# Merged streams in steps of two: maxima, value products and convolution transforms of an attention and long-convolution kernel

## The chip, the cores and the metric

The kernel runs as one program on one core of a Trainium2 chip. The metric is the device time of one launch in microseconds (us). Of the kernel before there are three timed runs: 1141.32 (the median), 1143.27 and 1141.15 us. A profile is one further execution, with the hardware's instruction records.

The core has five engines with a queue each, all in program order: PE (matrix products, with PEld for its weight loads), DVE (vector), ACT (activation), POOL (a second, slower vector engine, which also issues some DMAs) and SP (which here issues most DMAs). Products land in PSUM, eight banks of 128 partitions by 512 numbers; the other engines take them out of there.

## What is computed

Two independent halves, written side by side into one output of 2048 by 1152 numbers.

```python
# half A: attention, 32 heads of 18, a window of 256 keys, causal
qkv = x @ wqkv
scores = q @ k.T * 18 ** -0.5, masked to 0 <= i - j < 256
a = concat_heads(softmax(scores) @ v) @ wo
# half B: a convolution over the sequence, one filter of 2048 taps per channel (576 channels)
K = Re sum_n C[d,n] * dB[d,n] * exp(dt A[d,n] * l)
b = irfft(rfft(u, 4096) * rfft(K, 4096))[:2048] + u * Dskip
```

## The kernel before, in words

**Three parts in time.** First the projections `x @ wqkv` (`proj`), the taps of the filters (`tables`) and the first step of a two-step Fourier transform of `u` and of the taps (`s1_u`, `s1_k`) run, the results going to DRAM (`qd`, `vd`, `gx`, `gk`). Then, under a hand-written order, comes `attention` (line 758), which merges the attention with the rest of the convolution. Last, the part of the output product that had to wait for the last heads (`wo_rest`). The change touches only the second part.

**Attention.** There are 16 units (8 groups of 4 heads, 2 halves of the sequence), each cut into 6 items: two chunks `c` of 512 queries by three banks of the `BL` table (line 657). So there are 96 items, and 98 rounds of the loop in line 768. For each unit:

- `gmax` (line 627) finds, for blocks of 32 queries, the greatest score of each query, before the softmax. It copies the queries into a block-diagonal tile `qb` (DVE, line 632). Then for each of 32 blocks PE forms the scores of 4 heads by 2 products (line 640, weights of 128 rows by 64 columns) into one `ring` buffer, and DVE takes the maximum over up to 288 keys (line 643). A transpose on PE (line 648) and a scaling on DVE (line 650) turn the 32 columns of maxima into rows, which SP copies into the query tile (line 653).
- `scores` (line 662) forms an item's transposed scores, in two steps (head pairs `jp`), by products with 64 rows by 128 columns of weights (line 676) into `stp`; ACT takes the exponential into `P` (line 678); after both steps POOL masks the blocks on the window's edge (line 687).
- `values` (line 690) runs two items later: for each of an item's one or two blocks, 4 products (one for each head, 8 instructions in the profile, since a product of 32-bit numbers is two) with 128 rows by 32 columns of weights (line 699), a step of the merge for each block. At the last bank ACT takes the sum out (line 707).
- `norm` (line 724) divides by the sums of the softmax: DVE lines 735, 738, 748, 751, PE line 747 (full-size weights), ACT line 749, POOL's DMAs line 755.

**Convolution.** `conv` (line 484) takes 16 pairs of frequencies, each in two halves `hs` of the channels. For one half: two transforms of `u` (`s2`, line 504, part `tx`, weights 128 by 64), each taken out to `X` by ACT (line 527); the transform of the taps, real part `kr` and imaginary part `ki` (line 504, part `tk`), each multiplied straight from PSUM by two DVE products (lines 530, 531 and 534, 535); POOL adds the terms to `Y` (lines 539, 540). The inverse transform of the half before follows: two products with full-size weights (line 511), each taken out by ACT (line 512) into `ho`, which goes to DRAM `h`. After all 16 pairs, a second loop of 16 passes `qd` reads `h` back (`loadh`, line 551: 4 DMAs on SP's queue, 4 of `u` on POOL's), does the last transform (line 577), adds `u * Dskip` (DVE line 579; POOL line 573 forms the product) and writes the output by 4 DMAs from SP, given to `after` for the next round.

**What sets the order.** Each of these is a Python generator; a `yield` ends a step. `merge` (line 82) always calls the stream that has done the smallest share of its steps, the first in the list on a tie. In each round the list is: `scores` with 2 steps, a part of `gmax` with 5 or 6, `values` with 2, a part of `conv` with 2 or 3 (222 over 96 rounds, line 796), and later the output product `wo_first`, `wo_part`. The order in which the steps are called is the order of the instructions in each engine's queue. `share` (line 102) spreads a total over rounds. `after` and `begin` (lines 114, 118) hold a DMA back to the start of a later round.

**The buffers in between.** All products but `scores` and `values` take their PSUM bank from one pool, `ring`, with three buffers, in turn (`stp` has two of two banks each, `ops` one): a product waits until the buffer used three allocations ago has been read out. `fy` and `fs` hold the convolution's SBUF tiles, two of each name.

## Time and profile before

| what | value |
|---|---|
| median of three runs | 1141.32 us (1141.15 to 1143.27) |
| the profiled execution | 1142.89 us, of which the span of the instructions is 1141.2 us |
| first part (to the filters' transform) | to about 522 us |
| merged part: maxima of the first unit | 522 to 545 us |
| rounds 0 to 81 | 545 to 1004 us |
| rounds 82 to 97 (the convolution's last loop among them) | 1004 to 1112 us |
| the last output products | 1112 to 1141.2 us |
| instructions of line 640, 699, 504, 511 (all on PE) | 1024, 1408, 512, 128 |

How the profile is read: a timeline row gives start, duration, engine, line, operation, the tile written and the tiles read, the weights' shape (rows `*` columns) for PE, the shape of the result, and the number of instructions merged into the row; `[0.41 <-DVE t L535]` says that the engine stood idle for 0.41 us before it and which instruction released it. PE's ends are modelled, and rows overlap a little, so PE's rate is read from start to start. A group's row gives a line's total busy time, the mean duration in ns, and the idle time before it with its releasers. A row of waits gives who waited for whom: the total in us, how often, and the longest. The chain that ended last is followed back from the last instruction, at each step to what released it. In the table by stage each row has, for each engine, busy us and the number of instructions, then the granted clock of PE, the busy share of the DMA engines and GB/s.

### The profile page before, as it was taken

What the parts mean: (1) busy time and instruction counts of PE and PEld (TensorE: products, weight loads), DVE (VectorE), ACT (ScalarE), POOL (GpSimd) and SP (SyncE); (2) the same over time, 40 slices, a digit from 0 to 9 for tenths busy, and PEclk for the clock granted to TensorE, in tenths of its full rate; (3) what the DMA queues carried; (4) which work ended last, traced back from release to release, by engine and by line L of the source; (5) the groups of instructions that cost most, each with busy time, mean ns of one, the idle gap of its engine ahead of it and who ended that gap; (6) DMA issues with size and microseconds to landing.
All of it is one profiled execution on the core that took longest, in us unless ns stands there. A gap on an engine that the chain in (4) does not pass through costs nothing.

```text
span 1141.2 us, 27005 instructions
## 1 busy us (share of the span) xinstructions
PE 921.1 (81%) x10412; PEld 450.9 (40%) x10412; DVE 717.9 (63%) x1805; ACT 624.2 (55%) x955; POOL 519.8 (46%) x618
## 2 busy tenths in 40 slices
PE   1535879887979789885888889889888999987876
PEld 0313436555545555532333333333333444433325
DVE  2879656866785562266667677787776566563344
ACT  1785778777878842231355555655555455544430
POOL 0014324442644330102355556666756555487860
PEclk9957989898989889998599998999999999999888
DMA  9564423433343325885153464544445334287753
GB/s 272 152 192 138 97 50 90 110 87 84 87 106 65 76 56 124 216 252 159 43 163 117 129 184 115 156 132 125 132 127 153 88 125 142 81 229 214 195 152 129
DMA packets 156186, 152.45 MB, mean 134 GB/s; under 512 B 37001, under 2 KB 134665, under 8 KB 155865
## 3 DMA queue, kind: packets, MB, share of 16 engines
q1 hardware_dynamic: 148488, 132.14, 42.3%
q0 software_dynamic: 6064, 14.60, 4.9%
q10 hardware_dynamic: 1504, 3.99, 1.3%
q8 instruction: 82, 1.34, 0.5%
q14 instruction: 48, 0.39, 0.1%
HBM read 89.27 MB, written 61.01 MB: 132 GB/s over the span
## 4 chain that ended last, share of the span: by engine, by line
PE 50%; DVE 19%; DMA 10%; ACT 9%; issue 7%; SPq 4%; POOL 1%; DVEq 0%; ACTq 0%; POOLq 0%
PE pp L176 8%; PE po L699 7%; PE r L504 6%; PE r L640 6%; PE r L893 4%; PE r L511 4%; PE ST L676 3%; PE pp L465 3%; PE kp L422 3%; PE r L747 3%; PE x L318 2%; DMA gk<-g 2%; DVE tr L362 2%; DMA K<-in_wqkv_dram 2%; DVE jk L643 1%
## 5 line engine op out<-in xcount | busy, mean ns | idle before, releaser
L643 DVE CUSTOM_DVE_ANT_0 jk<-r,bias 128x288 f32<-128x288 f32 (+7 forms) x512 | 206.5, 435 | 121.6 <-PE r L640 118.8
L678 ACT ACTIVATE P<-ST,esc 128x1024 f32<-128x1024 f32 (+1 forms) x192 | 203.3, 1059 | 93.9 <-PE ST L676 89.4
L384 POOL TENSOR_TENSOR m<-A,tr 128x1024 f32<-128x1024 f32 x72 | 149.6, 2099 | 194.1 <-PE kp L422 141.1
L687 POOL TENSOR_SCALAR_AFFINE_SELECT P<-P 128x512 f32<-128x512 f32 x240 | 158.1, 688 | 107.2 <-ACT P L678 105.0
L640 PE MATMUL r<-K,qb 128*64 128x288 f16 (+7 forms) x1024 | 134.9, 301 | 24.6 <-DVE t L531 5.9
L539 POOL TENSOR_TENSOR Y<-t,t 64x288 f32<-64x288 f32 x64 | 54.4, 849 | 149.8 <-DVE t L534 147.9
L699 PE MATMUL po<-P,V 128*32 128x256 f32 (+2 forms) x1408 | 118.8, 410 | 4.3 <-ACT osb L707 2.2
L640 PEld LDWEIGHTS <-qb 128*64 128x64 f16 x1024 | 61.0, 112 | 128.4 <-issue 78.6
L422 PE MATMUL kp<-Q,m 128*32 128x64 f32 x4608 | 87.9, 230 | 27.7 <-DVE Q L405 10.6
L422 PEld LDWEIGHTS kp<-Q,m 128*32 128x32 f32 x4608 | 75.0, 116 | 56.0 <-issue 40.4
L465 PE MATMUL pp<-ut,w 128*128 128x288 f32 x128 | 52.4, 535 | 42.8 <-DMA ut<-in_u_dram 25.8
L676 PE MATMUL ST<-Q,K 64*128 64x384 f16 (+2 forms) x704 | 75.8, 286 | 2.2 <-DMA Q<-m 2.1
L241 DVE SCALAR_TENSOR_TENSOR qst<-pp,qst 128x512 f16<-128x512 f32 x36 | 24.7, 686 | 64.2 <-ACT qst L240 64.1
L749 ACT ACTIVATE oh<-osb 128x512 f16<-128x512 f32 x28 | 17.6, 630 | 78.9 <-DVE osb L748 78.9
L132 ACT ACTIVATE g<-pp 128x288 f32<-128x288 f32 (+1 forms) x84 | 34.5, 447 | 39.7 <-DMA gk<-g 19.9
L504 PE MATMUL r<-tx,w 128*64 128x288 f32 x256 | 47.0, 448 | 10.8 <-DMA tx<-gx 9.2
L540 POOL TENSOR_TENSOR Y<-t,t 64x288 f32<-64x288 f32 x64 | 53.2, 831 | 3.8
L465 PEld LDWEIGHTS pp<-ut,w 128*128 128x128 f32 x128 | 28.8, 244 | 63.4 <-issue 26.4
L511 PE MATMUL r<-Y,i 128*128 128x288 f32 x128 | 50.7, 480 | 3.7 <-DVE m L643 1.5
L330 ACT ACTIVATE ab<-k 128x512 f32<-128x512 f32 (+1 forms) x54 | 31.9, 591 | 36.5 <-DVE k L329 36.0
L176 PE MATMUL pp<-xh,wh 128*128 128x512 f16 x180 | 47.8, 387 | 1.2 <-DVE xh L233 1.2
L504 PE MATMUL r<-tk,w 128*64 128x288 f32 x256 | 46.4, 443 | 2.8 <-DVE m L643 1.0
(176 smaller groups left out, 1814.3 us busy)
## 6 DMA issues: line engine op xcount, KB each, us to landing
gx<-g SPq DMA_DIRECT2D x32, 288.0 KB
qd<-qst SPq DMA_DIRECT2D x72, 128.0 KB
gk<-g SPq DMA_DIRECT2D x16, 576.0 KB
tx<-gx SPq DMA_DIRECT2D x16, 576.0 KB
tk<-gk SPq DMA_DIRECT2D x16, 576.0 KB
h<-ho SPq DMA_DIRECT2D x16, 576.0 KB
raw<-in_xT_dram SPq DMA_DIRECT2D x16, 512.0 KB
Q<-qd SPq DMA_DIRECT2D x32, 216.0 KB
```

Of the source, the lines that this page charges most:

```text
L176: self.nc.tensor.matmul(ps, u, v, start=(i == 0), stop=(i == len(ops) - 1))
L384: self.nc.gpsimd.tensor_tensor(m, A[:, ch, a0:a0 + 8].unsqueeze(3).to_broadcast(sh), tr[:, ch, part, 0:8].unsqueeze(2).to_broadcast(sh), o ...
L422: nc.tensor.matmul(kp[32 * st:32 * st + 32, c % 2 * JJ2 + j, :], m[:, ch, a0:a0 + 32], Q[:, ch, term % 2, :], start=(term == 0), stop=(ter ...
L465: nc.tensor.matmul(ps, self.w1[:, part, :], src[:, o:o + k], start=True, stop=True)
L504: nc.tensor.matmul(ps[64 * par:64 * par + 64], w2[:, par, 64 * part:64 * part + 64], t[:, 2 * hs:2 * hs + 2, par, :], start=True, stop=True)
L511: nc.tensor.matmul(ps, i1[:, par, :], Y[par], start=True, stop=True)
L640: nc.tensor.matmul(ps[64 * b:64 * b + 64, :n], self.qb[:, b, t, :], d["K"][:, b, k0:k0 + n], start=True, stop=True, skip_group_check=True)
L643: nc.vector.tensor_tensor_reduce(out=jk[:, :n], in0=ps[:, :n], in1=self.bias[:, 288 - n:], scale=1.0, scalar=-3e38, op0=OP.add, op1=OP.max ...
L676: nc.tensor.matmul(ps[:, u, o:o + n], d["K"][h, jp, k0:k0 + 128], d["Q"][h, jp, q0:q0 + n], start=True, stop=True, skip_group_check=True)
L678: nc.scalar.activation(pt[:, 2 * jp:2 * jp + 2, lo:hi], ps[:, :, lo:hi], AF.Exp, scale=self.esc)
L687: nc.gpsimd.affine_select(v, v, pattern=[[0, 4], [sg, 128]], compare_op=OP.is_ge, fill=0.0, base=-1 if far else 0, channel_multiplier=-sg)
L699: nc.tensor.matmul(self.po[32 * j:32 * j + 32, t0 * 128:t1 * 128], V[:, kb * 76 + 19 * j:kb * 76 + 19 * j + 32], pt[:, j, o:o + (t1 - t0) ...
```

## The change

`gmax` now does two blocks in a step: both pairs of products first, then both maxima; its number of steps goes from 35 to 19. `values` does both blocks of an item in one step. In `conv` the two transforms `tx` are formed one after the other and taken out together, likewise the two of `tk` (with all four DVE products behind them), the two inverse products, and the two halves of a pass of the last loop; the steps go from 234 to 117 and the empty steps ahead of `loadh` and of the last loop from 3 and 5 to 2 and 3. The shares in `attention` are set to the new numbers of steps. No product, no element-wise operation and no transfer is added or taken away, and no pool gets more buffers.

```diff
         def inverse(fp, hs, i1, Y, ho):
+            pair = []
             for par in range(2):
-                ps = ring()
-                nc.tensor.matmul(ps, i1[:, par, :], Y[par], start=True, stop=True)
-                nc.scalar.activation(ho[:, par, hs * 288:hs * 288 + 288], ps, AF.Copy)
-                yield
+                pair.append(ring())
+                nc.tensor.matmul(pair[par], i1[:, par, :], Y[par], start=True, stop=True)
+            for par in range(2):
+                nc.scalar.activation(ho[:, par, hs * 288:hs * 288 + 288], pair[par], AF.Copy)
+            yield
...
+                pair = [s2(cu["w2"], cu["tx"], p, hs) for p in range(2)]
                 for p in range(2):
-                    nc.scalar.activation(X[:, p], s2(cu["w2"], cu["tx"], p, hs), AF.Copy)
-                    yield
-                kr = s2(cu["w2"], cu["tk"], 0, hs)
+                    nc.scalar.activation(X[:, p], pair[p], AF.Copy)
+                yield
+                kr, ki = [s2(cu["w2"], cu["tk"], p, hs) for p in range(2)]
                 tt(t1[:, 0], X[:, 0], kr, op=OP.mult)
                 tt(t2[:, 1], X[:, 1], kr, op=OP.mult)
-                yield
-                ki = s2(cu["w2"], cu["tk"], 1, hs)
                 tt(t2[:, 0], X[:, 1], ki, op=OP.mult)
                 tt(t1[:, 1], X[:, 0], ki, op=OP.mult)
...
+        for _ in range(2):
+            yield
+        nx = [loadh(0), loadh(1)]
         for _ in range(3):
-            yield
-        nx = [loadh(0), loadh(1)]
-        for _ in range(5):
             yield
...
+            pair = [ring() for hf in range(2)]
             for hf in range(2):
-                ps = ring()
                 for k in range(2):
-                    nc.tensor.matmul(ps[64 * k:64 * k + 64], self.i2, hp[:, k, hf * 288:hf * 288 + 288],
+                    nc.tensor.matmul(pair[hf][64 * k:64 * k + 64], self.i2, hp[:, k, hf * 288:hf * 288 + 288],
                                      start=True, stop=True)
-                tt(y[:, hf * 288:hf * 288 + 288], ps, ut[:, hf * 288:hf * 288 + 288], op=OP.add)
-                yield
+            for hf in range(2):
+                tt(y[:, hf * 288:hf * 288 + 288], pair[hf], ut[:, hf * 288:hf * 288 + 288], op=OP.add)
+            yield
...
+        pair = []
         for t in range(32):
             ps = self.p["ring"].tile([128, 512], F32, name="r")
...
-            jk = self.p["m"].tile([128, 288], F32, name="jk")
-            nc.vector.tensor_tensor_reduce(out=jk[:, :n], in0=ps[:, :n], in1=self.bias[:, 288 - n:], scale=1.0,
-                                           scalar=-3e38, op0=OP.add, op1=OP.max, accum_out=m[:, t:t + 1])
+            pair.append((t, n, ps))
+            if t % 2 == 0:
+                continue
+            for t, n, ps in pair:
+                jk = self.p["m"].tile([128, 288], F32, name="jk")
+                nc.vector.tensor_tensor_reduce(out=jk[:, :n], in0=ps[:, :n], in1=self.bias[:, 288 - n:], scale=1.0,
+                                               scalar=-3e38, op0=OP.add, op1=OP.max, accum_out=m[:, t:t + 1])
+            pair = []
             yield
...
-            yield
+        yield
...
-        merge((self.gmax(0), 35), (part(conv, 12), 12))
+        merge((self.gmax(0), 19), (part(conv, 6), 6))
...
-                    g = 11
+                    g = 6
                 elif n < 3:
-                    g = 11
+                    g = 7 - n
...
-                    g = share(0, 33, 6)
+                    g = share(0, 17, 6)
                 elif 3 < n < 87:
-                    g = share((n - 3) % 6, 33, 6)
+                    g = share((n - 3) % 6, 17, 6)
...
-                streams.append((self.values(*items[n - 2]), 2))
-                k = share(n - 2, 222, 96)
+                streams.append((self.values(*items[n - 2]), 1))
+                k = share(n - 2, 111, 96)
                 streams.append((part(conv, k), k))
```

More of the change, by code (lines that the diff above doesn't have):

```diff
@@ L560, in loadh @@
             return hp, ut
-        for _ in range(3):
+        for _ in range(2):
             yield
         nx = [loadh(0), loadh(1)]
-        for _ in range(5):
+        for _ in range(3):
             yield
```

## The prediction, as put on record before the result

> **What bounds the kernel now.** I read the page's list of engines first, then the chain that ended last in two stretches, then the table by stage.
>
> ```profile
> PE 921.1 (81%) x10412; PEld 450.9 (40%) x10412; DVE 717.9 (63%) x1805; ACT 624.2 (55%) x955; POOL 519.8 (46%) x618
> ```
> ```profile
> 545.00:1004.00 459.00, 408.30 (x3485) 163.74 (x3485) 311.72 (x1146) 248.89 (x349) 268.40 (x390) 0.96 0.44 127
> 1004.00:1112.00 108.00, 88.70 (x730) 34.63 (x729) 46.39 (x119) 48.24 (x62) 85.84 (x131) 0.91 0.76 201
> ```
> ```profile
> by line: PE po L699 15.6%; PE r L640 13.1%; PE r L504 13.1%; PE r L511 9.2%; issue 7.7%; PE ST L676 7.7%; PE r L747 5.5%; PE r L893 5.0%; DVE jk L643 2.8%; DVE qb L632 2.7%; ACT P L678 1.8%; DVE t L531 1.8%; DVE t L535 1.6%; DMA Q<-m 1.5%;
> ```
> ```profile
> by line: SPq L123 11.4%; DMA out_dram<-t 10.3%; DMA tx<-h 10.3%; SPq L555 9.3%; PE r L747 7.5%; PE r L577 7.2%; PE r L893 7.2%; PE po L699 6.8%; issue 5.9%; DMA Q<-m 5.6%; DVE spread L738 2.7%; DVE t L579 2.6%; PE ST L676 2.3%; SPq L732 2.2
> ```
>
> The merged part is two stages. In rounds 0 to 81 (545 to 1004 us, the first chain) PE is busy 408 of 459 us, and its lines with "issue" hold over three quarters of the chain: a microsecond off PE's queue there is mostly a microsecond off the time. In rounds 82 to 97 (the second chain) SP's queue and the DMAs of `h` and of the output lead, with the DMA engines at 0.76: PE's work counts little. Nothing of the change lies before 522 us or after 1112 us.
>
> **What PE gains.** No product goes, but the steps follow each other differently. What a step costs beyond its columns is read from start to start on PE:
>
> ```profile
> 641.00 0.34 PE L676 MATMUL ST<-Q,K 64*128 64x384 f16 x2
> 641.26 0.31 PE L640 MATMUL r<-K,qb 128*64 128x288 f16 x2
> 641.51 0.64 PE L699 MATMUL po<-P,V 128*32 128x256 f32 x8
> 642.08 0.71 PE L504 MATMUL r<-tk,w 128*64 128x288 f32 x4
> 642.61 0.41 PE L640 MATMUL r<-K,qb 128*64 128x288 f16 x4
> 642.96 0.34 PE L676 MATMUL ST<-Q,K 64*128 64x384 f16 x2
> ...
> 644.51 0.75 PE L511 MATMUL r<-Y,i 128*128 128x288 f32 x2
> 645.20 0.44 PE L640 MATMUL r<-K,qb 128*64 128x288 f16 x4
> ...
> 653.43 0.31 PE L640 MATMUL r<-K,qb 128*64 128x288 f16 x2
> 653.61 0.71 PE L504 MATMUL r<-tk,w 128*64 128x288 f32 x4
> ```
> ```profile
> 707.41 0.71 PE L504 MATMUL r<-tx,w 128*64 128x288 f32 x4 [0.20 <-DVE m L643]
> 708.05 0.34 PE L676 MATMUL ST<-Q,K 64*128 64x384 f16 x2
> ```
>
> One block of maxima ahead of values takes 0.25 us (641.26 to 641.51), two in a row 0.35 (642.61 to 642.96): the second adds 0.10. One block ahead of a transform, whose weights have the same shape 128*64, takes 0.18 (653.43 to 653.61). A transform takes 0.53 ahead of maxima (642.08 to 642.61), the same shape, and 0.64 ahead of scores of another shape (707.41 to 708.05). So what costs is not the end of a step but the change of the weights' shape: 0.07 to 0.15 us each, and I take 0.11, the transform's own difference.
>
> [...]
>
> Following the rule of `merge` through the first part's last step and rounds 0 to 97, I count the places where the shape changes (64*128 scores, 128*64 maxima and transforms, 128*32 values and the maxima's transpose, full size for the inverse, `norm` and the output product). Round 34 is, before: scores, maxima, values, inverse, two maxima, scores, maxima, values, inverse, two maxima: 10 runs of one shape. After: scores, two maxima, both values, both inverses, two maxima, scores, two maxima: 7. In all there are 832 changes before and 648 after; up to round 81, 706 and 556. That is 150 x 0.11 = 16.5 us where PE leads, and 34 more after it, 3.7 us, which I count at nothing, because SP's queue and the DMAs cover them.
>
> Two full-size products in a row gain a little more, since the second's weights can load behind the first:
>
> ```profile
> 469.08 6.07 PE L465 MATMUL pp<-K,w 128*128 128x384 f32 x18 [1.89 <-ACT vst L252]
> 475.86 2.20 PE L465 MATMUL pp<-K,w 128*128 128x384 f32 x6 [0.71 <-ACT g L132]
> ```
>
> Twelve more instructions take 3.87 us, 0.32 each for 384 columns, so 0.24 for 288 and 0.48 for an inverse of two; alone it takes 0.69 (644.51 to 645.20). The pair saves 0.21, of which 0.11 is counted; 32 x 0.10 = 3.2 us. PE's sum where it leads: **19.7 us**; between 12 and 26 with 0.07 to 0.15.
>
> **What is late next: the transform of the taps.** With three buffers, the second product of a pair waits for the first reading of the pair before. PE's waits in 545 to 1004 us:
>
> ```profile
> PE r L648 <- DVE m L643: 12.6, 14, 1.4
> PE r L640 <- DVE t L531: 4.6, 10, 0.5
> PE r L640 <- DVE m L643: 4.2, 8, 1.8
> ...
> PE r L747 <- DVE t L535: 3.1, 4, 0.8
> PE r L640 <- DVE t L535: 2.7, 7, 0.5
> ...
> PE r L747 <- DVE t L531: 1.7, 2, 0.9
> ```
> ```profile
> 740.55 0.31 PE L640 MATMUL r<-K,qb 128*64 128x288 f16 x2
> 740.79 0.64 PE L699 MATMUL po<-P,V 128*32 128x256 f32 x8
> 741.36 0.71 PE L504 MATMUL r<-tk,w 128*64 128x288 f32 x4
> ```
> ```profile
> 740.05 0.45 DVE L531 TENSOR_TENSOR t<-X,r 128x288 f32<-128x288 f32 x1
> 740.41 0.45 DVE L643 CUSTOM_DVE_ANT_0 jk<-r,bias 128x288 f32<-128x288 f32 x1
> ...
> 742.12 0.45 DVE L534 TENSOR_TENSOR t<-X,r 128x288 f32<-128x288 f32 x1 [0.49 <-PE r L504]
> 742.49 0.45 DVE L535 TENSOR_TENSOR t<-X,r 128x288 f32<-128x288 f32 x1
> ```
>
> DVE starts 0.76 us after a transform's start (741.36 to 742.12), its products follow at 0.37, each lasts 0.45, and PE goes on 0.05 after the end (740.50 to 740.55). In the new order `kr` and `ki` start at 0 and 0.53, and the next pair of maxima, usually directly behind (23 of 32 times), at 1.06. Its second product needs the buffer of `kr`, which DVE's second product frees at 0.76 + 0.37 + 0.45 + 0.05 = 1.63; it could have started at 1.18: 0.45 lost. The pair after it, one scores step (0.26) later, needs `ki`, free after four products at 2.37, and could start at 2.13: 0.24. Behind the waiting maxima stand scores and values, with the exponential on ACT waiting for them. 0.69 x 32 halves = 22 us, against 4.6 + 3.1 + 2.7 + 1.7 = 12.1 in the rows above, which these replace: **10 us lost**; between 0 (norms and other work let DVE and PE meet elsewhere) and 22. The transpose's wait, 12.6, stays: it stands behind the last two maxima before and after.
>
> **Edits at nothing.** A pair of maxima, start 0: DVE takes the first from 0.35 on (PE's row lasts 0.31), frees it at 0.35 + 0.45 + 0.05 = 0.85. The second product of the next pair, one scores step later, comes at 0.35 + 0.26 + 0.12 = 0.73 to 0.80 (a scores step of four products takes 0.32). So it just meets its buffer; I take 0 to 0.1 of the 106 such places as part of the range, and what happens if DVE runs late is the first rival. The pairs `X` and `ho` put two ACT instructions in a row; the exponential of the next scores queues behind them, and ACT has 459 - 249 = 210 us free. Joined values need their second block's mask earlier:
>
> ```profile
> 730.07 3.96 POOL L687 TENSOR_SCALAR_AFFINE_SELECT P<-P 128x512 f32<-128x512 f32 x5
> ```
> ```profile
> 730.95 0.42 PE L699 MATMUL po<-P,V 128*32 128x128 f32 x8
> 731.31 0.71 PE L504 MATMUL r<-tx,w 128*64 128x288 f32 x4
> ...
> 733.09 0.85 PE L699 MATMUL po<-P,V 128*32 128x384 f32 x8
> ```
>
> This is the tightest place that I found: the first three masks of these five end about 732.0 (five in 3.96, with a gap), the second block would follow at 731.3 instead of 733.1, 0.8 late; elsewhere the masks end over a microsecond before the first block. I take 1 us, at most 14 units x 0.8 = 11. In the convolution's last loop the loads move from round 81 to 82 (8 DMAs on SP's queue, 8 on POOL's, behind that round's own), the first pass from round 83 to 85, the last stays in 97, and each output DMA stays two rounds or so behind its pass. SP's queue issues the same number. I take nothing, between 4 us won (16 passes in 12 rounds instead of 14) and 8 lost (a round and a half of 5.5 us later, if the loop of loads and writes bounds the end).
>
> **The sum.** 19.7 - 10 - 1 = 8.7, say 9 us, from the profiled execution's 1142.89 us (span 1141.2 and 1.7 around it): 1134. The median, 1141.32, is 1.6 lower, so I forecast **1132 us** as its counterpart, with its own range 1121 to 1139.
>
> **Rivals.**
>
> *Maxima in lock-step, slower.* If DVE is one operation late (0.37 us) when a pair arrives, each of the 106 pairs separated by scores alone loses 0.30: 32 us, and 1132 + 32 = 1164; late at half of them, 1148. It decides from about 0.3 of them on. For it: DVE has 312 us in the stage, 71% of the time left after PE's saving, and comes in bursts of 4 and 6. Against: 4.2 us of such waits now, at the same depth of three. [...] No row shows DVE as the bound of this stage yet.
>
> *The last loop takes it.*
>
> ```profile
> DVE t L579 <- DMA out_dram<-t: 20.7, 4, 11.7
> ```
>
> DVE waits here for output writes to land before it may reuse a tile. With passes starting a round and a half later the end moves by up to 8 us: 1140, against the range 1136 to 1146.
>
> *PE's sum comes whole.* The waits behind the taps' transform only move; then 1141.3 - 20 = 1121, down to 1112 with 0.15 for each change and the 3.7 us of the later rounds.
>
> *It does not do what it says.* PE is no longer the bound as soon as it is relieved, DVE sets the pace through `ring` at today's rate: 1141.
>
> **Chances.** Forecast 0.48, all of it faster. PE's sum whole 0.14, faster. Last loop 0.14: 0.04 faster, 0.05 within, 0.05 slower. Lock-step 0.21: 0.01 within, 0.20 slower. Nothing moves 0.03, within. Faster by over 0.2% (2.3 us, about what a measurement of this kernel can tell from no change) 0.66, within 0.09, slower 0.25. For 8 in 10 I leave out the upper half of the lock-step and the lowest of PE's sum: 1113 to 1152.
>
> **What would show it.** Right: 1024 products of line 640 in runs of four where they now stand in twos; PE's starts from block to block at 0.35 for a pair and about 1.0 for an item's values; rounds 0 to 81 about 9 us shorter; waits of line 640 for 531 and 535 up from 7 to some 17 us. Wrong: waits of 640 for 643 far above 4 us (lock-step); a stage to round 81 that is 20 us shorter (the waits only moved); a shorter first stage with a longer one from round 82 on (the last loop). A transform ahead of maxima that no longer takes 0.53 would fell the price of a change of shape.

## The result, and the profile after

The kernel after takes 1112.31 us (median of four runs, 1108.92 to 1116.83) beside 1141.24 of the kernel before (four runs, 1139.94 to 1143.27): a ratio of 0.9747 with a 95% interval of 0.971 to 0.9785, 29 us faster, where the forecast was 9. The profiled execution took 1108.92 us (span 1107.2), 34.0 less than that of before; it is the fastest of its four, so the stages below sum to more than the medians.

The page's list of engines for the kernel after:

```profile
PE 891.3 (80%) x10412; PEld 458.8 (41%) x10412; DVE 716.2 (65%) x1805; ACT 622.0 (56%) x955; POOL 532.8 (48%) x618
```

PE is busy 30 us less with the same 10412 instructions; no other engine moves by more than 13. The table by stage shows where. Its rows are called rounds 0 to 11, 12 to 80, 81 to 94, and 95 to the end; they start at the first scores product of rounds 0 and 12 and, half a round early and alike in both kernels, at the second scores step of rounds 80 and 94. After the window come its length, the busy time of PE, PEld, DVE, ACT and POOL, the granted clock, the DMA share and GB/s. Before:

```profile
544.66:608.94 64.28, 56.77 (x447) 22.07 (x447) 41.05 (x182) 31.45 (x42) 32.19 (x46) 0.82 0.34 101
608.94:997.94 389.00, 346.85 (x2992) 139.29 (x2992) 266.56 (x949) 215.01 (x305) 231.77 (x338) 0.98 0.45 131
997.94:1087.46 89.52, 74.78 (x654) 30.43 (x652) 38.39 (x117) 42.71 (x53) 75.89 (x117) 0.92 0.80 214
1087.46:1141.20 53.74, 38.39 (x270) 21.07 (x268) 24.95 (x36) 8.59 (x13) 15.72 (x23) 0.87 0.43 132
```

After:

```profile
542.20:597.98 55.78, 49.01 (x441) 21.38 (x441) 39.36 (x180) 30.42 (x41) 31.53 (x44) 0.94 0.38 113
597.98:970.45 372.47, 334.16 (x3010) 148.94 (x3009) 264.83 (x956) 215.62 (x306) 245.03 (x340) 0.99 0.48 137
970.45:1053.60 83.15, 71.06 (x644) 32.48 (x642) 37.39 (x110) 40.91 (x51) 73.45 (x112) 0.96 0.79 216
1053.60:1107.20 53.60, 36.50 (x269) 22.06 (x268) 27.21 (x38) 8.99 (x14) 19.66 (x28) 0.90 0.51 154
```

So 2.5 us are won ahead of round 0, 8.5 in rounds 0 to 11, 16.5 in rounds 12 to 80, 6.4 in rounds 81 to 94, nothing after. A second profiled execution of each kernel (`before_again`, `after_again`) gives 6.8, 15.9 and 9.3 us for the same three stages. In rounds 12 to 80 PE's busy column falls by 12.7 and what is not busy from 42.2 to 38.3. The chain that ended last, 542 to 976 us of the kernel after:

```profile
by line: PE po L707 12.6%; issue 10.9%; PE r L643 10.4%; PE r L504 9.2%; PE r L512 6.9%; PE ST L684 6.9%; PE r L755 6.2%; PE r L901 5.7%; DVE jk L650 4.0%; DVE t L535 2.0%; DMA raw<-in_wo_dram 1.9%; DVE t L533 1.9%; DVE spread L746 1.9%; PO
```

PE still leads, with less: 504 falls from 13.1 to 9.2%, the inverse (now 512) from 9.2 to 6.9, maxima (643) from 13.1 to 10.4, while "issue" and DVE's maxima (650) rise. PE's waits in the same window, and a stretch of its timeline:

```profile
PE r L656 <- DVE m L650: 11.4, 14, 0.8
PE r L643 <- DVE t L534: 8.9, 23, 0.5
PE po L707 <- ACT osb L715: 5.8, 10, 0.8
PE po L707 <- POOL P L695: 2.6, 3, 1.5
...
PE r L755 <- DVE t L536: 1.0, 2, 0.5
PE r L643 <- DVE t L536: 1.0, 4, 0.4
```
```profile
603.50 1.07 PE L707 MATMUL po<-P,V 128*32 128x384 f32 x16
604.50 1.19 PE L504 MATMUL r<-tk,w 128*64 128x288 f32 x8
605.52 0.29 PE L643 MATMUL r<-K,qb 128*64 128x288 f16 x2
606.23 0.31 PE L643 MATMUL r<-K,qb 128*64 128x288 f16 x2 [0.41 <-DVE t L534]
606.47 0.28 PE L684 MATMUL ST<-Q,K 64*128 64x256 f16 x2
606.96 0.69 PE L643 MATMUL r<-K,qb 128*64 128x288 f16 x4 [0.20 <-DVE t L536]
```

An item's values take 1.00 (603.50 to 604.50), two transforms 1.02, 0.51 each ahead of maxima of the same shape. Then the pair of maxima waits, exactly where the prediction put it: its second product for the first buffer of the taps (0.41), the next pair for the second (0.20).

What PE's rows cost in rounds 12 to 80, each taken from its start to the next row's start less the idle time before that one, and the idle time by who waits (the sum has also the maxima's transpose, 2.4 and 2.5 us, and the output product, 23.3 in both):

```
              values  inverse  transforms  scores  maxima  norm  | sum   | idle
before         75.0    38.2      58.6      46.0    81.9   24.2  | 350.0 | 39.0
after          66.5    33.5      56.9      45.2    84.5   25.2  | 338.0 | 34.5
idle before     2.5     2.1       3.8       0.0    14.3    5.9  (the maxima's transpose 10.4)
idle after     10.2     3.4       2.3       0.0     8.6    1.2  (the maxima's transpose  8.9)
```

So PE's rows gave 12.0 us and the idle time 4.5; between the second executions it is 10.8 and 5.1. Maxima, formed two blocks at a time now, did not become cheaper but dearer. And the waits changed hands: values wait more, maxima and `norm` less.

### The profile page after: what moved, and what is told of

Same layout as the page of the kernel before. It is cut to its first block, busy times and chain, and to the rows that moved or that the text cites. A ratio compares the mean times of both kernels' runs of the same rounds, so it can differ in the third digit from the quotient of the medians.

```text
span 1107.2 us, 26979 instructions
## 1 busy us (share of the span) xinstructions
PE 891.3 (80%) x10412; PEld 458.8 (41%) x10412; DVE 716.2 (65%) x1805; ACT 622.0 (56%) x955; POOL 532.8 (48%) x618
## 4 chain that ended last, share of the span: by engine, by line
PE 43%; DVE 20%; DMA 12%; ACT 10%; issue 8%; POOL 5%; SPq 1%; DVEq 0%; ACTq 0%; POOLq 0%
PE pp L176 8%; PE po L707 5%; PE r L901 5%; PE r L643 4%; PE r L504 4%; PE pp L465 3%; PE r L755 3%; PE ST L684 3%; PE r L512 3%; PE kp L422 3%; DMA gk<-g 2%; DVE jk L650 2%; PE x L318 2%; DVE tr L362 2%; POOL P L695 2%
## 5 line engine op out<-in xcount | busy, mean ns | idle before, releaser
L650 DVE CUSTOM_DVE_ANT_0 jk<-r,bias 128x288 f32<-128x288 f32 (+7 forms) x512 | 197.6, 434 | 109.1 <-PE r L643 108.2
L695 POOL TENSOR_SCALAR_AFFINE_SELECT P<-P 128x512 f32<-128x512 f32 x240 | 171.4, 743 | 108.2 <-ACT P L686 105.8
L643 PE MATMUL r<-K,qb 128*64 128x288 f16 (+7 forms) x1024 | 128.2, 297 | 17.7 <-DVE t L534 9.3
L707 PE MATMUL po<-P,V 128*32 128x256 f32 (+2 forms) x1408 | 100.6, 397 | 16.5 <-ACT osb L715 6.4
L422 PE MATMUL kp<-Q,m 128*32 128x64 f32 x4608 | 86.4, 227 | 27.2 <-DVE Q L405 11.4
L540 POOL TENSOR_TENSOR Y<-t,t 64x288 f32<-64x288 f32 x64 | 53.9, 842 | 107.6 <-DVE t L535 55.3
L643 PEld LDWEIGHTS <-qb 128*64 128x64 f16 x1024 | 57.3, 109 | 98.2 <-issue 54.8
L422 PEld LDWEIGHTS kp<-Q,m 128*32 128x32 f32 x4608 | 73.5, 114 | 55.4 <-issue 42.4
L707 PEld LDWEIGHTS po<-P,V 128*32 128x32 f32 x1408 | 35.9, 110 | 53.7 <-issue 35.6
L541 POOL TENSOR_TENSOR Y<-t,t 64x288 f32<-64x288 f32 x64 | 56.2, 878 | 3.8
L330 ACT ACTIVATE ab<-k 128x512 f32<-128x512 f32 (+1 forms) x54 | 31.9, 590 | 37.5 <-DVE k L329 37.1
L504 PE MATMUL r<-tx,w 128*64 128x288 f32 x256 | 40.6, 437 | 10.2 <-DMA tx<-gx 9.5
L176 PE MATMUL pp<-xh,wl 128*128 128x512 f16 x180 | 48.5, 394 | 0.0
L176 PEld LDWEIGHTS <-wh 128*128 128x128 f16 x324 | 31.7, 100 | 39.6 <-issue 6.4
```

Source lines behind the costliest of these rows:

```text
L176: self.nc.tensor.matmul(ps, u, v, start=(i == 0), stop=(i == len(ops) - 1))
L422: nc.tensor.matmul(kp[32 * st:32 * st + 32, c % 2 * JJ2 + j, :], m[:, ch, a0:a0 + 32], Q[:, ch, term % 2, :], start=(term == 0), stop=(ter ...
L504: nc.tensor.matmul(ps[64 * par:64 * par + 64], w2[:, par, 64 * part:64 * part + 64], t[:, 2 * hs:2 * hs + 2, par, :], start=True, stop=True)
L541: nc.gpsimd.tensor_tensor(Y[par][64:128], t1[sl, 1], t2[sl, 1], op=OP.add)
L643: nc.tensor.matmul(ps[64 * b:64 * b + 64, :n], self.qb[:, b, t, :], d["K"][:, b, k0:k0 + n], start=True, stop=True, skip_group_check=True)
L650: nc.vector.tensor_tensor_reduce(out=jk[:, :n], in0=ps[:, :n], in1=self.bias[:, 288 - n:], scale=1.0, scalar=-3e38, op0=OP.add, op1=OP.max ...
```

## The experiments

**Theory** after the result: the joined steps save PE's changes of shape as priced, and the waits behind the taps only change hands. **Rivals**: one join alone brings the gain, by where it puts work in a round; the clock brings part of it; the length of DVE's readings, not PE, holds maxima.

**The three parts alone**, each on the kernel before with its functions and shares as in the change (one line of each is shown: `values_only`, `maxima_only`, `conv_only`), and the kernel before once more.

```diff
-                streams.append((self.values(*items[n - 2]), 2))
+                streams.append((self.values(*items[n - 2]), 1))
...
-        merge((self.gmax(0), 35), (part(conv, 12), 12))
+        merge((self.gmax(0), 19), (part(conv, 12), 12))
...
-                k = share(n - 2, 222, 96)
+                k = share(n - 2, 111, 96)
```

> Only the values are done in one step; maxima and convolution stay as before. Theory, changes of the weights' shape: counted by the merge rule, 726 changes instead of 832 (106 fewer; the whole change has 184 fewer and won 29 us, 0.16 each with everything in it). At 0.12 us each 13 us faster, 1128; with 0.16, 17 faster. Rival, number of steps (each step that is joined saves the same, whatever stands beside it): 80 of 448 joined steps, 29 x 80 / 448 = 5 us faster, 1136. PE's time for the values themselves should fall by some 8 us in both, since the second block follows the first.

> Only the maxima are done in twos. Theory, changes of shape: 780 instead of 832, 52 fewer, 6 us faster, 1135 (8 with 0.16). Rival, number of steps: 256 of 448, 17 us faster, 1124. A third, the lock-step that was feared (the second product of a pair waits for the first maximum of the pair before), would make this one slower than before, up to 32 us, since here a pair stands beside single scores, values and transforms.

> Only the convolution's transforms, inverses and last passes are done in twos. Theory, changes of shape: 774 instead of 832, 58 fewer, 7 us, and 3 for the weights of the inverse: 10 us faster, 1131. Rival, number of steps: 112 of 448, 7 us faster, 1134. Waits of maxima on the products with the taps (lines 530 to 536) should not be above the 12 us of before if the prediction's second waiting place is empty. If the last stage (rounds 82 to 97) is shorter here by about 6 us, that gain belongs to the convolution's last loop.

> The kernel before, unchanged, for a second profile: is the low granted clock of 0.82 in rounds 0 to 11 (0.94 after the change) a property of that kernel or of that execution? If of the kernel, the clock here is again below 0.87 in 545 to 609 us and the stage takes 63 to 65 us; if of the execution, it can be above 0.90 and the stage takes about 57 to 60.

Values 1138.59 us, ratio 0.998 (0.9957 to 1.0003); maxima 1136.4, 0.9962 (0.9933 to 0.9991); the convolution 1120.21, 0.9805 (0.9771 to 0.984). Against 1141.22 that is 2.6, 4.8 and 21.0, together 28.4: within the intervals the parts add to the whole, and three quarters are the convolution's, twice what its expectation gave the shapes; the first can't be told from no change and lies below both its prices (13 and 5 us). On PE's rows in rounds 12 to 80 they don't add: values alone take 65.9 us for 75.0 there, maxima alone 75.1 for 81.9, but maxima in the kernel after 84.5. So the price of a shape holds (601 changes became 525 with values alone, 8.4 us by 0.11, and 9.1 measured on their rows), and time hardly follows it. The kernel before again took 1142.93, with rounds 0 to 11 in 63.4 us at a clock of 0.84, as in the first profile (64.3 at 0.82).

**Which join of the convolution?** A first run took the taps' join off the kernel after.

```diff
-                kr, ki = [s2(cu["w2"], cu["tk"], p, hs) for p in range(2)]
+                kr = s2(cu["w2"], cu["tk"], 0, hs)
                 tt(t1[:, 0], X[:, 0], kr, op=OP.mult)
                 tt(t2[:, 1], X[:, 1], kr, op=OP.mult)
+                yield
+                ki = s2(cu["w2"], cu["tk"], 1, hs)
...
-                k = share(n - 2, 111, 96)
+                k = share(n - 2, 141, 96)
```

> The changed kernel, but the transform of the taps in two steps again, each with its two vector products (shares set to 149 steps, the last loop begins in the same round). Prediction's price for the joined step: 10 us lost by it, so 1102 here. Theory now: the joined step costs nothing that a split one does not cost too, because PE waits at 23 places 0.4 us for the real part's second product and hardly ever for the imaginary part's; changes of shape 476 against 474 in rounds 12 to 80: 1110 to 1116.

1128.13 us, 0.9904 (0.988 to 0.9929): slower than the kernel after, but it settles nothing, because the new shares let the last loop begin two rounds later (its first product in round 87, at 1014.3 us, in place of round 85, at 994.0). Four further runs keep the convolution's work in its rounds: `taps_split` is the same edit with `k` mapped step for step to the old rounds, `taps_only`, `x_only` and `inv_only` put one join each on the kernel before.

```diff
+                p, q = [e * 4 // 3 if e <= 96 else e + 32 for e in (6 + r * 111 // 96 for r in (n - 2, n - 1))]
+                k = q - p
```

> The kernel after with the taps' transform in two steps again, the last loop kept in its rounds (the earlier run taps_single had let it slip). Prediction's price: 10 us less, 1102. Theory now: the join costs nothing here; 1110 to 1116, with waits for line 534 gone and as many for the norm product or the maxima back.

> The kernel before with kr and ki formed one after the other and all four DVE products behind them (5 steps for a half in place of 6), the rounds of the convolution's work and its last loop kept. Prediction's price: 10 us of waits more, less some 2 us for changes of shape, so 1149, with waits for the taps' DVE products at about 22 us in rounds 12 to 80. Theory now: the waits only change hands (the norm product's 5.9 us go), 1136 to 1142.

> The kernel before with the two transforms of u joined alone. By shapes: at most 32 steps fewer, 0.11 us each: 1137 to 1139. If ACT's two copies in a row hold back the exponential, 1141 or more.

> The kernel before with the two inverse products joined alone. By the prediction's price 32 x 0.21 = 6.7 us less: 1134; the stage table has 38.2 us of inverse rows before and 33.5 after, which says 4.7 in rounds 12 to 80 and 1.7 in rounds 0 to 11. If joins of the convolution pay by fewer steps in the merge, x_only, inv_only and taps_only win alike, 5 to 7 us each, and add to 21.

`taps_split` 1120.95 us, 0.9854 (0.9832 to 0.9875); `taps_only` 1134.21, 0.9949 (0.9929 to 0.9969); `x_only` 1136.99, 0.9976 (0.9961 to 0.9991); `inv_only` 1140.14, 1.0009 (0.9986 to 1.0031). The taps' join, which the prediction charged with 10 us, wins: 5 us on the kernel before, and without it the kernel after is 9 us slower by the medians (1112 to 1121) and 12 by the ratios, each to the kernel before measured beside it. Both of my numbers for `taps_split` (1102 and 1110 to 1116) were missed, and both for `taps_only` (1149 and 1136 to 1142). The waits of `taps_split` for the taps' products, rounds 0 to 81:

```profile
PE r L645 <- DVE t L534: 7.1, 15, 0.8
PE r L645 <- DVE t L538: 4.1, 11, 0.5
PE r L757 <- DVE t L538: 1.5, 2, 0.8
PE r L512 <- DVE t L538: 1.2, 2, 0.7
```

13.9 us with the taps split, 10.9 joined (the three rows of the kernel after above; 0.4 more stands ahead of its inverse). Split, each of the two transforms meets its own wait; joined, nearly only the first does. The inverse's join is the opposite case: its rows fall from 37.1 us in the kernel before again to 33.5, the idle time of maxima rises from 14.8 to 22.9, and the time stays (1134 was expected). In rounds 12 to 80 maxima wait 5.8 us there for ACT's copy of `X`, where the kernel before has 1.6, and 5.3 for the first product of the taps, where it has 2.7. X, taps and inverse alone add to 6 us (2.2 + 5.0 - 0.9) of the convolution's 21.

**Its last loop.** In the kernel after the loop's first pass comes two rounds later (85 in place of 83), and both halves of a pass are one step. Here the halves are split again, at the same pace.

```diff
-            pair = [ring() for hf in range(2)]
             for hf in range(2):
+                ps = ring()
...
-                k = share(n - 2, 111, 96)
+                k = share(n - 2, 111, 96) * (2 if n > 84 else 1)
```

> The changed kernel, but each pass of the convolution's last loop in two steps of half a pass, at the same pace (twice the number of steps a round from round 85 on). Theory: the 6 us won from round 81 on belong to the pass in one step, since its writes need only one half's wait; then 1116 to 1118. Rival: they come from the later start of the loop and from PE's shorter rounds, whatever the step; then 1112 within 2 us.

1110.24 us, 0.9744 (0.9717 to 0.9772): the joined halves are worth nothing that can be told (1116 to 1118 was the theory's). The later start is left. DVE and PE of the kernel before, where `norm` meets the loop:

```profile
1044.41 0.82 DVE L579 TENSOR_TENSOR t<-r,t 128x288 f32<-128x288 f32 x2 [3.77 <-DMA X<-in_u_dram]
1056.93 0.46 DVE L579 TENSOR_TENSOR t<-r,X 128x288 f32<-128x288 f32 x1 [11.69 <-DMA out_dram<-t]
1057.30 0.34 DVE L735 RECIPROCAL den<-den 128x32 f32<-128x32 f32 x1
1057.68 2.90 DVE L738 TENSOR_TENSOR spread<-den,heads 128x1024 f32<-128x1024 f32 x1
```
```profile
1052.95 1.23 PE L577 MATMUL r<-tx,i 128*64 128x288 f32 x4 [3.51 <-DMA tx<-h]
1060.72 2.04 PE L747 MATMUL r<-spread,heads 128*128 128x512 f32 x2 [6.55 <-DVE spread L738]
```

DVE stands 11.69 us before an add until an output write has landed; `norm`'s `spread` is queued behind that add, and PE waits 6.55 us for it. In the kernel after DVE waits even longer in sum, but in shorter pieces, and PE never waits for `spread` there:

```profile
DVE t L581 <- DMA out_dram<-t: 29.2, 7, 6.7
```

PE's idle time ahead of `norm`, rounds 81 to 94, is 8.2 us before, 9.0, 7.5 and 7.1 in `x_only`, `inv_only` and `taps_only` (loop where it was), 0.6 to 0.9 in `conv_only`, `taps_split` and the kernel after (loop later); these rounds take 88.7 to 89.5 us in the first group and 82.5 to 84.8 in the second. So about 6 us go with where the loop begins. That the later start is their cause is argued, not shown: no run moves the loop alone, `values_only` takes 85.8 with the loop where it was, and in `taps_single`, where it begins two rounds later still, `norm` waits only 0.2 us and the rounds take 92.1.

**Place in the round.** Is the convolution best between the other streams? Here its part of a round comes behind all of them.

```diff
-                streams.append((part(conv, k), k))
+                late = part(conv, k)
...
             merge(*streams)
+            for _ in late:
+                pass
```

> The changed kernel with the same steps, but each round's step or two of the convolution run at the end of the round, behind the last maxima. Changes of the weights' shape: 460 in rounds 12 to 80 against 474, so by the shapes alone it is 1 to 2 us faster, 1111. Theory, place in the round: the kernel before has a step of the convolution among the last three steps ahead of 29 of 30 products of the norm (line 755 here, 747 before), the changed one ahead of 9, and the waits before this product fell from 5.9 to 1.2 us in rounds 12 to 80, with others that hang on the two vector products behind the transform of the taps. Put at the end again the waits must come back: idle time of PE in rounds 12 to 80 up from 34.5 to over 40 us, time 1118 or more.

1105.13 us, 0.9694 (0.9666 to 0.9723); `loop_halves` on the same chip had 0.9744. My theory that the gain needs the convolution's steps away from `norm` fell: this is faster still. PE's waits up to round 82:

```profile
PE r L643 <- DVE m L650: 15.1, 16, 1.7
PE r L643 <- DVE qb L634: 10.3, 9, 2.1
PE ST L684 <- DMA Q<-m: 2.4, 2, 2.1
PE r L656 <- DVE m L650: 0.8, 1, 0.8
```

The transpose's 11.4 us and the values' 8.4 are all but gone; DVE's maxima are waited for instead. Of the 14 transposes, 13 now stand behind a product of the convolution, where all 14 stood behind maxima. The values still stand behind maxima or scores; why they wait no more is not shown. Idle time in rounds 12 to 80 is 21.8 us, after 34.5.

**The clock at round 0.** Granted clock and PE's busy time in steps of 5 us, before and after:

```profile
540.00:545.00 5.00, 2.62 (x18) 1.20 (x17) 3.59 (x15) 2.10 (x3) 0.18 (x1) 0.93 0.23 63
545.00:550.00 5.00, 4.60 (x34) 2.21 (x33) 3.52 (x23) 2.49 (x3) 1.24 (x2) 0.50 0.38 117
550.00:555.00 5.00, 4.92 (x32) 1.74 (x31) 4.20 (x22) 1.80 (x2) 0.63 (x1) 0.50 0.21 64
555.00:560.00 5.00, 4.46 (x26) 1.55 (x24) 2.71 (x12) 0.44 (x1) 0.00 (x0) 0.50 0.00 0
```
```profile
545.00:550.00 5.00, 4.71 (x32) 2.08 (x30) 4.86 (x27) 1.87 (x3) 1.37 (x3) 0.61 0.53 160
550.00:555.00 5.00, 4.04 (x36) 1.58 (x34) 4.20 (x19) 1.12 (x1) 0.97 (x2) 1.00 0.00 0
```

Ahead of round 0 PE waits for the copies of the maxima, in both kernels 2.13 us, and the clock falls from 1.00 to 0.50; in these executions it stays low for over 15 us before and some 7 after. How long is not a property of the kernel: in their second executions it is about 10 us in both (first `before_again`, then `after_again`).

```profile
550.00:555.00 5.00, 4.91 (x32) 1.69 (x29) 4.14 (x22) 1.80 (x2) 0.63 (x1) 0.55 0.19 55
555.00:560.00 5.00, 3.42 (x32) 1.49 (x29) 3.89 (x17) 1.11 (x1) 0.64 (x1) 1.00 0.00 0
```
```profile
550.00:555.00 5.00, 4.92 (x36) 2.00 (x36) 3.61 (x20) 1.80 (x2) 0.63 (x1) 0.63 0.06 16
```

The row of before that has the gap:

```profile
544.66 1.07 PE L676 MATMUL ST<-Q,K 64*128 64x384 f16 x2 [2.13 <-DMA Q<-m]
```

One run fills that gap:

```diff
+        warm = self.p["ring"].tile([128, 512], F32, name="r")
+        for _ in range(5):
+            self.nc.tensor.matmul(warm[:, :288], self.same, self.bias, start=True, stop=True)
```

> The kernel before with one thing added: five full-size products into a ring buffer that nobody reads, ahead of round 0, where PE stands idle for 2.1 us (542.5 to 544.7 us) and after which the granted clock falls from 1.00 to 0.50. Theory (clock): that gap makes the clock fall, and the low clock costs rounds 0 to 11 of the kernel before 6 to 8 us more than the kernel after; filled, the clock stays near 1.00 from 545 us on, rounds 0 to 11 take 56 to 59 us in place of 64.3, the median is 1133 to 1136. Rival (steps): the joined steps alone shorten rounds 0 to 11, the clock is granted by something else; the rounds stay at 63 to 64 us and the median at 1140 to 1142.

1139.71 us, 0.9973 (0.9949 to 0.9996). The clock holds until about 560 us (1.00, then 0.98 in the last 5 us) and is 0.50 in the 5 us behind:

```profile
545.00:550.00 5.00, 4.37 (x34) 1.76 (x33) 4.72 (x29) 2.27 (x3) 1.40 (x3) 1.00 0.56 174
550.00:555.00 5.00, 4.01 (x36) 1.49 (x35) 4.01 (x19) 1.11 (x1) 0.47 (x1) 1.00 0.01 5
555.00:560.00 5.00, 3.38 (x32) 1.51 (x29) 4.38 (x18) 1.91 (x2) 3.42 (x5) 0.98 0.01 2
560.00:565.00 5.00, 4.53 (x26) 1.49 (x29) 2.40 (x12) 2.83 (x5) 3.94 (x6) 0.50 0.17 49
```

Rounds 0 to 11 take 60.7 us at 0.94, the clock of the kernel after, whose rounds take 55.8. So of the 8.5 us some 3.6 are the clock's in these two executions and 5 the steps'; in the median the clock is worth 1.5 to 3. Both forecasts of the theory, 56 to 59 us and 1133 to 1136, were missed, and both of the rival.

The clock differs from execution to execution elsewhere too. Over the 85 timed executions of the kernel before, on five chips, a mean granted clock that is 0.01 higher goes with 1.6 to 3.4 us less. The mean is 0.925 there, 0.927 in the first four runs of the kernel after and 0.937 in its later five, 0.934 in `conv_only`, 0.933 in the two runs `half_max` and `before_half` that follow, 0.924 in `inv_half`. So hardly any of the 29 us need be the clock's. About 2 us can be in the 21 of `conv_only`, in the 15 that `before_half` wins below, and between `before_half` and `inv_half`.

**Who holds maxima?** DVE reads half as long, on the kernel after, on the kernel before, and on the latter with the inverse's join.

```diff
-  out=jk[:, :n], in0=ps[:, :n], in1=self.bias[:, 288 - n:], scale=1.0,
+  out=jk[:, :n // 2], in0=ps[:, :n // 2], in1=self.bias[:, 288 - n:288 - n + n // 2], scale=1.0,
```

> The kernel after, whose DVE reads only the first half of each block's keys for the maximum (it leaves out the other half of the search); PE's products are all there. Theory (ring): in the kernel after, maxima's rows on PE hold hidden waits for DVE's reading, which is why the parts do not add (18.8 us of PE's work saved by the parts alone, 10.6 together); with the reading at about 0.25 us in place of 0.45, maxima's rows in rounds 12 to 80 fall from 84.5 us to 75 to 78, the waits behind line 650 and line 534 fall by half, and the median is 1092 to 1100. Rival (PE alone): the rows are long for a reason of PE's own; the median stays at 1108 to 1113.

> The kernel before, whose DVE reads only the first half of each block's keys for the maximum (it leaves out the other half of the search), as half_max did with the kernel after (1111 to 1096). Theory (PE and DVE hold each other through the three buffers already before the change): 1125 to 1132. Rival (PE alone bounds the kernel before, as the prediction had it): 1138 to 1141.

> before_half with the two inverse products joined, as inv_only joined them on the kernel before (0 us won of 6.4 us of PE's rows saved). Theory (saved PE time is given back as waits for DVE): with DVE's reading halved the join pays, 4 to 7 us below before_half. Rival (the join costs elsewhere, in ACT's two copies in a row): within 2 us of before_half.

`half_max` 1096.16 us, 0.9623 (0.9598 to 0.9649), where the kernel after, measured beside it, had 0.9738 (0.9715 to 0.9762); `before_half` 1124.75, 0.9868 (0.9844 to 0.9893); `inv_half` 1126.73, 0.9893 (0.9868 to 0.9918). Both kernels gain 15 us, although DVE is busy 71% of its time at most: the premise that PE alone bounds this stage fell, for the kernel before too. DVE's maxima in rounds 12 to 80, after and then with half the keys (the second window is half a round longer):

```profile
L650 DVE CUSTOM_DVE_ANT_0 jk<-r,bias 128x288 f32<-128x288 f32 (+4 forms) x367 | 144.6, 439 | 82.7 <-PE r L643 82.0
```
```profile
L650 DVE CUSTOM_DVE_ANT_0 jk<-r,bias 128x144 f32<-128x144 f32 (+4 forms) x370 | 96.3, 297 | 109.9 <-PE r L643 105.9 <-issue 0.2 <-PE ST L684 0.2
```

One reading falls from 439 to 297 ns, DVE waits more for PE than before, and yet PE's maxima take 76.1 us in place of 84.5. So the 84.5 held waits too short to be told as idle rows. The starts show them. In rounds 12 to 80, of 358 blocks of maxima for which the reading that frees their buffer can be told, 139 start within 0.11 us of its end; only 25 of these have an idle row. With half the keys it is 89 and 25. From the first block of a pair to the second PE takes 0.161 us with maxima alone joined, 0.194 in the kernel after, 0.171 with half the keys, at 184 pairs; so it is mostly the second block of a pair that just meets its buffer.

In the kernel before the place of the 15 us is not found. There this step takes 0.161 us and 0.149 with half the keys, and in rounds 12 to 80 the rows of values, inverse, scores and maxima fall alike, by 3 to 4%, while the clock there is 1.00 in that execution and 0.98 in the first of the kernel before.

The waits that are told moved too. PE's, in the kernel after with half the keys, to the end of round 81:

```profile
PE r L643 <- DVE t L534: 9.2, 23, 0.5
PE po L707 <- POOL P L695: 7.3, 6, 2.3
PE r L656 <- DVE m L650: 6.8, 14, 0.5
```

The transpose's wait falls from 11.4 to 6.8, the taps' stays (my text had it fall too), and the masks on POOL come forward, from 2.6 to 7.3.

`inv_half` is no faster than `before_half`: that halving DVE's reading would make the inverse's join pay fell with it. Its inverse rows fall by 4.7 us and maxima's idle time rises by 5.4: for ACT's copy of `X` from 0.8 to 3.5, for the first product of the taps from 2.7 to 5.4, for DVE's maxima from 3.7 to 5.0. That bears out the rival in part, ACT's copies in a row.

**One join more**: `scores` in one step for both head pairs.

```diff
             nc.scalar.activation(pt[:, 2 * jp:2 * jp + 2, lo:hi], ps[:, :, lo:hi], AF.Exp, scale=self.esc)
-            yield
+        yield
```

> One more join on top of the change: the scores of both head pairs in one step. Changes of shape fall from 474 to 343 in rounds 12 to 80 and from 648 to 472 in all. Theory, shapes at 0.11 us: 19 us faster than the changed kernel if no new wait comes, 1093. Rival: both buffers of the scores must be free at once, so PE waits for the exponentials of the round before (1.06 us each, two a round): slower than the changed kernel, 1120 or more, with waits of the scores on ACT that are zero now.

1121.0 us, 0.9842 (0.9812 to 0.9872): slower than the kernel after. PE's changes of shape in rounds 12 to 80 fall from 474 to 342 and the rows of scores by 9.5 us, but maxima's rows rise to 88.5 and the idle time to 42.7; PE's waits up to round 81:

```profile
PE r L643 <- DVE t L534: 9.9, 25, 0.5
PE r L643 <- DVE t L536: 6.7, 16, 0.5
PE r L643 <- DVE m L650: 3.5, 10, 0.6
PE r L643 <- ACT X L530: 3.4, 12, 0.6
```

Without a scores step between two pairs of maxima the second wait (for 536) and the lock-step (for 650), 1.0 us and none in the kernel after, are there: 6.7 and 3.5. The rival's reason, scores waiting for ACT's exponential, does not show.

**The kernel after again, and the fastest version**: `conv_at_end` with the five products of `before_warm`.

> The kernel after unchanged: 1109 to 1114, the clock back at 1.00 by 550 us, rounds 0 to 11 in 55 to 57 us. If the clock at the start of round 0 is chance, rounds 0 to 11 take 60 us or more here, and the time follows.

> The kernel after with the convolution's part of a round put behind all other streams (as in the run conv_at_end, 0.9694 of the kernel before) and the five products of before_warm ahead of round 0. Theory (clock): 1100 to 1103, since its rounds 0 to 11 ran at 0.91 and win 2 to 4 us. Rival (steps): 1105, as conv_at_end did. Either is below the kernel after in the same call, 1112, by 6 us or more; if it is not, the gain of conv_at_end was chance.

1111.42 us, 0.9738 (0.9715 to 0.9762), rounds 0 to 11 in 56.6 us at 0.91, though the clock is back at 1.00 only after 550 us (0.63 from 550 to 555); and 1103.16 us, 0.9673 (0.9653 to 0.9693), 8 us below the kernel after on the same chip. Its rounds 0 to 11 take 55.4 us at 0.94, `conv_at_end` 56.0 at 0.91; the five products did not keep its clock at 1.00 (0.88 from 545 to 550 us, 0.78 from 550 to 555). Whether they add to `conv_at_end` (1105.13, measured at another time) can't be told.

## Why the prediction was too small

- **PE's sum where it leads, 19.7 us.** The price of a change was right: 0.51 for a transform ahead of maxima (0.53 said), 1.00 for an item's values (about 1.0 said), an inverse pair from 38.2 to 33.5 us, 0.17 a pair (0.21 said). In rounds 12 to 80, 601 changes became 474; 127 x 0.11 and 27 x 0.10 for weights are 16.7, and 12.0 came (10.8 between the second executions). That weights load behind a product is in the trace of before: from 469.08 us PEld's 18 loads take 5.46 us, beside the 6.07 us of their 18 products on PE. Most of what is missing is in maxima, next point.
- **Pairs of maxima, 0 to 0.1 at 106 places.** The upper end, 10.6 us, nearly holds: 84.5 us where maxima alone have 75.1, and 76.1 with DVE's reading halved. This is the lock-step rival in small; its big form (32 us) did not come while scores stand between the pairs.
- **"What is late next", 10 us lost: the step that failed.** It multiplied both waits, 0.45 and 0.24, by all 32 halves, and set the 22 us against 12.1 to be replaced. The first wait came as described, at the 23 places counted, with 0.39 each, 8.9 in all; the second is nearly empty, 1.0 for maxima and 1.0 for `norm`. So joined taps wait 10.9 us, less than before, and the join wins 5 us on the kernel before and 9 to 12 in the kernel after where 10 were charged. With 1 us less of such waits in place of 10 more, this step is 11 of the 20 us missed. By its own sign of being wrong, a stage to round 81 that is 20 us shorter because the waits only moved, the prediction fails: that stage is 27.5 us shorter.
- **Joined values, 1 us.** The values' waits rose from 2.5 to 10.2 us in rounds 12 to 80. The masks, which I looked at, have 2.6 of them; more is ACT's taking the sum out (5.8 up to round 81), which I didn't price.
- **Last loop, 0 (4 won to 8 lost).** 6 won; I quoted the 11.7 us of DVE's wait as a price of the later start and did not look who was queued behind it. It was `norm`, and in the runs with the later start its wait is nearly gone; that the start alone does it is not shown.
- **Rounds 0 to 11** were treated like all others. Their low clock, 0.82, was averaged away in the one row that I read for 545 to 1004 us, 0.96: 1.5 to 3 us of the median. The steps' 5 us there are more than the stage's share of the forecast 9.
- **The rivals.** The time is the lower end of "PE's sum comes whole", and its mechanism, waits that only move, holds for the taps. But PE's sum did not come whole; the first rounds, the last loop and fewer waits filled the place, so that its time was met is luck. "Does not do what it says" has half a truth: DVE does hold maxima through `ring` in the kernel after, and the kernel before too gains 15 us from a shorter reading.
- **Open**: why the convolution's joins are worth more together. Alone the three give 6 us and the loop's place 6; 21 came. In rounds 12 to 80 `norm` waits 1.2 us with all of them, 6.0, 5.8 and 2.6 with one; that is part of it, not all. Open too is where the kernel before wins its 15 us from the shorter reading.

## What to carry to other kernels

Where a few PSUM buffers stand between engines, as the three of `ring` here, PE's saved time need not be the kernel's (`inv_only`: 3.6 us off PE's rows, 1140.14 us beside 1139.22): price a join by the buffers' next reader as well, count a wait only as often as the trace has its pattern, not once for each loop pass, and set against it the waits that the join takes away. Compare rows of two profiles only with their granted clocks beside them. To see whether an engine that is 70% busy holds another, halve its work in a run (DVE's reading of the maxima here, at 71%: 15 us) and look at the other's starts. Of a long wait, look first at who is queued behind it.

## What the runs showed of the hardware

The granted clock fell from 1.00 to 0.50 in an idle time of PE of 2.13 us, in both kernels. In the kernel before it stayed low for over 15 us in one execution, in which PE's rows were busy 4.46 to 4.92 of each 5 us, and for about 10 us in another; in the kernel after for some 7 and about 10. With the gap filled (`before_warm`) the clock stayed at 1.00 until 555 us, was 0.98 from 555 to 560, with 3.38 of these 5 us busy, and 0.50 from 560 to 565; in the run with the convolution at the end of the round (`end_warm`), the same filling did not hold it (0.88 from 545 to 550 us).
